# Windowed and coarse attention before two MLPs on one core: input loads put ahead of weights, value sums merged, and mask and spreading as matmuls for three half-batches

## The chip, the cores and the metric

The kernel runs on one core of a Trainium2 chip. The metric is device time in microseconds (us) from the start to the end of one execution; the median of several runs is given. The core has a matmul engine (TensorE, here PE, with its weight loads PEld), a vector engine (VectorE, DVE), a scalar engine (ScalarE, ACT), a general engine (GpSimd, POOL) and a queue engine (SyncE, SP) that issues transfers. PE writes its results to the accumulator memory PSUM; DVE and ACT read PSUM and the main on-chip memory SBUF. Each engine works through its own queue in order.

## What is computed

```python
B, H, S, D = 4, 8, 576, 64
def _attn_ref(q, k, v):
    factor = 4
    ...
    q_d = q.reshape(B, H, Sd, factor, D).mean(axis=3)      # likewise k_d, v_d
    out_d = sm_attn(q_d, k_d, v_d)
    out_up = np.repeat(out_d, factor, axis=2)
    mask = np.abs(pos[:, None] - pos[None, :]) < factor
    scores = scale * np.matmul(q, k.transpose(0, 1, 3, 2))
    scores = np.where(mask, scores, -1000000000.0)
    ...
    return (out_up + out_local).astype(np.float32)

def _moe_ref(x, w_in, w_out):                              # x: 2304 x 512, d_ff 2048
    h = x @ w_in
    return ((h * np.cos(h)) @ w_out).astype(np.float32)

def _moe2_ref(x, w_a, w_b, w_out):                         # d_ff 1536
    return ((x @ w_a) * (x @ w_b) @ w_out).astype(np.float32)

def reference(...):
    x = attn_out.transpose(0, 2, 1, 3).reshape(B * S, H * D)
    return _moe2_ref(x=_moe_ref(x, ...), ...)
```

An attention with two parts is followed by two MLPs. The local part lets each position see the three neighbours on either side; the coarse part runs a full attention over means of four positions, and each of its 144 results is repeated for four positions and added.

## The kernel before

The 2304 tokens are cut into eight half-batches u of 288 tokens (batch b, half of the sequence). The eight heads of a half-batch are taken as four pairs `hp`; two heads a = 0, 1 share the 128 partitions, 64 each.

For one pair, `down_sums` adds up four neighbouring columns of k and q, `local_scores` multiplies q and k in five windows of 64 positions into one PSUM tile (`att`), adds the mask with a DVE instruction (L214), takes the maximum (L218) and subtracts it (L219), and `down_scores` multiplies the summed q and k (L230). After the exponentials and the division (`local_norm`, `down_norm`) the weights are transposed on PE (`local_transpose`, `down_transpose`) and `attend` multiplies them with the values: four matmuls of 72 columns for the coarse part into columns 288 to 359 of the `att` tile (L315), ten for the windows into columns 0 to 287 (L322). `combine` copies the coarse result to SBUF on ACT (L332) and adds it, each column read four times, to the windows' result on DVE (L334); the sum `xf` is one 128-row block of x. `xsplit_hi` and `xsplit_lo` cut it into a high and a low half, `xh` (ACT) and `xl` (DVE, or POOL in u = 1 and 2). The values' sums over four positions, `vd`, are made by POOL in `sum_vs`, one head at a time: three additions of 72 x 128 elements from a tile `vs`.

Every product of the MLPs is made of three matmuls of 288 columns (`mm3`, L413 to L415) from high and low halves. A weight of 128 x 512 numbers comes as 64-bit floats of 0.5 MB (`wload`), and `wsplit` makes its halves: L107 and L111 on ACT, L108 and L109 on DVE, L112 on POOL. All 32 weights of the first MLP are split while its first four blocks run, at most eight loads ahead (`AHEAD`). A step g is one product `h` (one block of 128 hidden units for one half-batch), its `h cos(h)` on ACT and DVE (tile `gs`, L455 to L464), the halves `gh` and `gl`, and, three steps later, the four products `acc` with the second weight. The blocks run as u = 0 and u = 1 with hidden units 0 to 7, both with 8 to 15, and then u = 2 to 7 with all 16; the second MLP follows.

The attention of u = 0 stands ahead of the steps. That of u = 1 is spread over the first steps and that of u = 2 over steps 14 to 31, by tables of times `T1` and `T` (`unit_slots`); a planner then sorts each engine's instructions by what it expects to be ready, so that the order on an engine is not the order of the code. PSUM has two `att` tiles from u = 1 on; u = 0 borrows six more.

Of the kernel before, what the change touches and what calls it, by code (L numbers as in the profile page):

```python
# [36 lines left out]
C = {'AHEAD': 8, 'LEAD': 4, 'NPRE': 4, 'ND': 'ddd', 'XL': 'dpp', 'SUMS0': 'dddd', 'SUMS1': 'pppp', 'GLO': 8, 'FS': 8, 'S1': 0.7, 'G2': 14, 'LC': 0, 'DM': 2, 'LAG': 3, 'NGS': 3, 'MK': 0, 'SB': 'ddd', 'NL': 'dpp', 'W0': 0, 'W1': 0, 'W2': 0, 'W3': 0, 'NWV': 3, 'NGH': 4, 'XB': 8, 'YE': 6, 'CA': 2, 'NR': 4, 'PA': 1, 'LAG2': 2, 'PK': 1.0, 'GE': 'ad', 'NXF': 3, 'LP': 0, 'T': {'sums': [0, 0.5, 1.0, 3.0], 'ls': [0, 0, 0, 1.5], 'ds': [1, 1.5, 3, 4], 'ex': 6, 'ln': [6.0, 9.5], 'dn': [6, 7, 9, 10], 'dt': [7, 9.5, 11, 12], 'lt': [7.5, 8.5, 12.0, 13.5], 'at': [9.5, 9.5, 13.5, 14.5], 'xh': [11.0, 12.0, 15.0, 15.5], 'xl': [12.5, 13.5, 15.5, 15.5]}, 'T1': {'sums': [0, 0, 1.0, 2.0], 'ls': [0.5, 1.5, 2.5, 3.5], 'ds': [1, 1.5, 3, 4], 'ex': 5, 'ln': [5.5, 8], 'dn': [5.0, 6.0, 8.0, 9.0], 'dt': [6.0, 7.5, 10.0, 11.0], 'lt': [7.0, 8.0, 12.0, 12.0], 'at': [9, 9, 13, 14], 'xh': [9.0, 10.0, 13.0, 14.0], 'xl': [9.5, 11, 15, 15]}}  # L37
# [16 lines left out]
def kernel(ctx, tc, qT, kT, vw, vds, w_in, w_out, w_a, w_b, w_out2, out):  # L54
# [77 lines left out]
    def load_q(u, hp):  # L132
        if u < NU:
# [5 lines left out]
            sp.dma_start(out=t, in_=qT[b, hp, :, BASE[half]:BASE[half] + HALF])  # L139
            qt[u, hp] = t  # L140

    def load_v(u):
        for pr in range(HP // 2 if u < NU else 0):
# [539 lines left out]
```

## Time and profile before

| | |
|---|---|
| median of three runs | 1054.56 us (1050.47 to 1056.16) |
| the profiled execution | 1054.71 us, its span 1052.9 us |
| PE busy | 1009.0 us, 96% of the span |
| DVE, ACT, POOL busy | 543.1, 495.3, 188.1 us |
| moved by DMA | 72.97 MB |

The span runs from the first to the last instruction of the profiled execution. Busy time of PE is that of its matmuls; weight loads overlap them. An f32 matmul of the attention is recorded as two matmuls, so ten of them show as x20.

### The profile page before, as it was taken

The page shows a single profiled execution, that of the slowest core. Times are in us where ns is not written, and L with a number is a line of the kernel's source. Part 1 is how long each engine was busy: PE and PEld are TensorE (multiplying, and loading weights), DVE is VectorE, ACT ScalarE, POOL GpSimd, SP SyncE. Part 2 cuts the span into 40 slices and gives each one's busy share as a digit, 9 for nine tenths or more (in the row PEclk, how much of TensorE's full clock was granted, in tenths as well). Part 3 has the DMA queues.
Part 4 walks back from the last instruction along what each step waited for, and adds up shares of the span by engine and source line. Part 5 has one row for each costly group of instructions (what it writes and reads, how often), then busy time and mean ns, then how long its engine had stood idle before and what let it go on. Part 6 is the DMA issues. An engine that isn't in the chain of part 4 may idle for free.

```text
span 1052.9 us, 20576 instructions
## 1 busy us (share of the span) xinstructions
PE 1009.0 (96%) x8400; PEld 969.4 (92%) x8400; DVE 543.1 (52%) x1212; ACT 495.3 (47%) x1170; POOL 188.1 (18%) x215
## 2 busy tenths in 40 slices
PE   5978899999999999999999989999999999999998
PEld 4767789999999999999988979999999999999998
DVE  7788875674667756566488882222222222122211
ACT  4677766475665756657677562212121212122211
POOL 4868731000300003000033550000000001000000
PEclk9889999999999999999999999999999999999999
DMA  9545411301203012010174750001010102010000
GB/s 306 195 161 199 118 50 37 97 8 38 75 19 105 14 37 69 14 42 2 61 223 143 234 168 29 24 1 45 1 46 1 47 1 65 4 40 6 18 7 24
DMA packets 37919, 72.97 MB, mean 69 GB/s; under 512 B 4288, under 2 KB 22720, under 8 KB 37824
## 3 DMA queue, kind: packets, MB, share of 16 engines
q1 hardware_dynamic: 37824, 71.65, 21.3%
q8 instruction: 66, 1.08, 0.4%
q14 instruction: 29, 0.24, 0.1%
HBM read 61.01 MB, written 10.62 MB: 68 GB/s over the span
## 4 chain that ended last, share of the span: by engine, by line
PE 77%; POOL 6%; DVE 6%; issue 5%; DMA 3%; ACT 3%; SPq 0%; POOLq 0%; ACTq 0%; DVEq 0%
PE acc L413 10%; PE acc L414 9%; PE acc L415 9%; PE h L413 5%; PE h L414 5%; PE h L415 5%; PE pb L413 5%; PE pb L415 4%; PE pa L413 4%; PE pb L414 4%; PE pa L414 4%; PE pa L415 4%; POOL w L112 4%; PE att L322 2%; PE att L203 2%
## 5 line engine op out<-in xcount | busy, mean ns | idle before, releaser
L413 PE MATMUL acc<-gh,w 128*128 128x288 f32 x832 | 251.2, 302 | 2.0 <-DVE ev L449 1.5
L414 PE MATMUL acc<-gl,w 128*128 128x288 f32 x832 | 248.1, 298 | 3.5 <-DVE gl L472 1.7
L415 PE MATMUL acc<-gh,w 128*128 128x288 f32 x832 | 246.9, 297 | 0.0
L468 ACT ACTIVATE gh<-gs 128x288 fp32r<-128x288 f32 x224 | 99.3, 443 | 184.0 <-DVE gs L623 130.3
L623 DVE TENSOR_TENSOR gs<-a_sb,pb 128x288 f32<-128x288 f32 x96 | 43.5, 454 | 253.2 <-PE pb L415 253.2
L413 PE MATMUL h<-xh,w 128*128 128x288 f32 x512 | 159.0, 310 | 9.2 <-DVE gs L464 8.2
L413 PEld LDWEIGHTS acc<-gh,w 128*128 128x128 f32 x832 | 157.8, 190 | 7.0 <-issue 3.5
L414 PEld LDWEIGHTS acc<-gl,w 128*128 128x128 f32 x832 | 157.8, 190 | 5.6 <-DVE gl L472 2.9
L415 PEld LDWEIGHTS acc<-gh,w 128*128 128x128 f32 x832 | 157.9, 190 | 0.1
L415 PE MATMUL h<-xh,w 128*128 128x288 f32 x512 | 153.0, 299 | 1.4 <-POOL w L112 1.4
L472 DVE TENSOR_TENSOR gl<-gs,gh 128x288 fp32r<-128x288 f32 x216 | 115.7, 536 | 74.9 <-ACT gh L468 73.8
L414 PE MATMUL h<-xl,w 128*128 128x288 f32 x512 | 154.1, 301 | 0.0
L619 ACT COPY a_sb<-pa 128x288 f32<-128x288 f32 x96 | 38.3, 398 | 174.9 <-PE pa L415 174.8
L413 PEld LDWEIGHTS h<-xh,w 128*128 128x128 f32 x512 | 98.0, 191 | 16.6 <-DVE gs L464 14.2
L415 PEld LDWEIGHTS h<-xh,w 128*128 128x128 f32 x512 | 98.1, 192 | 1.7 <-POOL w L112 1.7
L414 PEld LDWEIGHTS h<-xl,w 128*128 128x128 f32 x512 | 98.0, 191 | 1.7 <-issue 1.7
L413 PE MATMUL pa<-xh,w 128*128 128x288 f32 x320 | 95.0, 297 | 2.5 <-ACT a_sb L619 2.5
L413 PE MATMUL pb<-xh,w 128*128 128x288 f32 x320 | 95.0, 297 | 2.2 <-DVE gs L623 2.2
L112 POOL TENSOR_TENSOR w<-raw,w 128x512 fp32r<-128x512 f32 x62 | 86.4, 1402 | 56.8 <-ACT w L111 56.6
L414 PE MATMUL pa<-xl,w 128*128 128x288 f32 x320 | 94.5, 295 | 0.0
L414 PE MATMUL pb<-xl,w 128*128 128x288 f32 x320 | 94.4, 295 | 0.0
L415 PE MATMUL pb<-xh,w 128*128 128x288 f32 x320 | 94.2, 294 | 0.0
(100 smaller groups left out, 1889.8 us busy)
## 6 DMA issues: line engine op xcount, KB each, us to landing
raw<-in_w_out_dram SPq DMA_DIRECT2D x28, 512.0 KB
raw<-in_w_in_dram SPq DMA_DIRECT2D x16, 512.0 KB
raw<-in_w_a_dram SPq DMA_DIRECT2D x12, 512.0 KB
raw<-in_w_b_dram SPq DMA_DIRECT2D x12, 512.0 KB
v<-in_vw_dram SPq DMA_DIRECT2D x16, 320.0 KB
q<-in_qT_dram SPq DMA_DIRECT2D x32, 146.0 KB
k<-in_kT_dram SPq DMA_DIRECT2D x16, 288.0 KB
vs<-in_vds_dram SPq DMA_DIRECT2D x32, 144.0 KB
```

Source lines behind the costliest of these rows:

```text
L112: lo_eng.tensor_tensor(out=t[:, 1], in0=lw.bitcast(F32), in1=t[:, 0].bitcast(F32), op=ALU.subtract)
L203: pe.matmul(p[r, W * w:W * w + W], qt[u, hp][r, off:off + W], kt[b, hp][r, BASE[half] + off:BASE[half] + off + W], start=not pem, stop=True,)
L322: pe.matmul(p[64 * a:64 * a + 64, xo:xo + n], vt[u, hp // 2][r, w, a], pt[u, hp // 2][r, w, 64 * a + qo:64 * a + qo + n], start=True, stop ...
L413: i = pe.matmul(ps_out, lh, rh, start=start, stop=False)
L414: pe.matmul(ps_out, lh, rl, start=False, stop=False)
L415: pe.matmul(ps_out, ll, rh, start=False, stop=stop)
L468: act.activation(out=gh[g], in_=gs[g], func=AF.Copy)
L472: eng.tensor_tensor(out=gl[g], in0=gs.pop(g), in1=gh[g].bitcast(F32), op=ALU.subtract)
L619: act.copy(out=a_sb, in_=pa)
L623: dve.tensor_tensor(out=gs[g], in0=a_sb, in1=pb, op=ALU.mult)
```

## The change

Six things change.

1. The loads ahead of the first step: SP issues the four key loads, one weight, two value tiles, a weight, and so on, and the query loads of u = 0 go to ACT's queue. Before, SP alternated keys, queries and four weights, and the value tiles came behind.
2. `load_vs` and `sum_vs` handle a pair of heads at a time: four transfers of 72 x 1024 numbers in place of eight of 72 x 512, and three additions of 72 x 256 elements in place of six of 72 x 128.
3. For u = 0 the sums of pairs 2 and 3 (`SUMS0`) go from DVE to POOL.
4. For u < 3 (`MK`) the mask is put into the PSUM tile by one bf16 matmul (identity times mask, 320 columns) ahead of the ten of q and k, which then add to it. The DVE addition L214 falls away, and maximum and subtraction read PSUM.
5. For u < 3 (`UP`) the coarse matmuls of `attend` read each weight column four times, and so write 288 columns where they wrote 72, straight into the columns of the windows' result, to which the window matmuls then add. `combine` only hands the PSUM tile on; `xsplit_hi` and `xsplit_lo` read it from PSUM, the latter on DVE for all of u < 3.
6. The queue memory kept for DMA descriptors is set to 1024 (`dynamic_dma_scratch_size`), and in u = 0 `local_scores` is written ahead of `down_sums`.

```diff
-C = {... 'SUMS0': 'dddd', ... 'MK': 0, ...}
+C = {... 'SUMS0': 'ddpp', ... 'MK': 3, 'UP': 3, ...}
...
-            o = vdt[b, hp][:, par]
+            t = vst.pop((u, hp))
+            o = vdt[b, hp] = at.tile([QD, 4, D], F32, tag="vd", name="vd", bufs=4)
             pool.tensor_tensor(out=o, in0=t[:, :, 0], in1=t[:, :, 1], op=ALU.add)
...
-                    start=not pem, stop=True,
+                    start=not pem, stop=not pem or w == NW - 1,
...
     def attend(u, hp):
+        up = u < C["UP"]
         for c in range(2):
             for a in range(2):
-                pe.matmul(
-                    p[64 * a:64 * a + 64, NB:NB + QD], vdt[b, hp][:, a, c], pd[u, hp][:, 2 * a + c],
-                    start=(c == 0), stop=(c == 1),
-                )
+                w = pd[u, hp][:, 2 * a + c]
+                o = p[64 * a:64 * a + 64, NB:NB + QD]
+                if up:
+                    o = p[64 * a:64 * a + 64, :NB].rearrange("p (s r) -> p s r", r=4)
+                    w = w.unsqueeze(2).to_broadcast([QD, QD, 4])
+                pe.matmul(o, vdt[b, hp][:, 2 * a + c], w, start=(c == 0), stop=(c == 1 and not up))
...
-                    start=True, stop=True,
+                    start=not up, stop=not up or w == NW - 1,
...
     def combine(u, hp):
         p = opsum.pop((u, hp))
+        if u < C["UP"]:
+            xf[u, hp] = p[:, :NB]
+            return
...
-                     (T["xl"][hp], xsplit_lo, u, hp, pick("XL", u))]
+                     (T["xl"][hp], xsplit_lo, u, hp, dve if u < C["UP"] else pick("XL", u))]
...
-            load_q(0, hp)
-            if hp < C["NPRE"]:
-                load_next(None)
-        for hp in range(HP):
-            for par in range(2):
-                load_vs(0, hp, par)
-        load_v(0)
-        for _ in range(C["AHEAD"] - C["NPRE"]):
+            load_q(0, hp, act)
+        load_next(None)
+        load_vs(0, 0)
+        load_vs(0, 1)
+        load_next(None)
+        load_v(0, 0)
+        load_vs(0, 2)
+        load_vs(0, 3)
+        load_v(0, 1)
+        for _ in range(C["AHEAD"] - 2):
             load_next(None)
         for hp in range(HP):
+            local_scores(0, hp)
             down_sums(0, hp)
-            local_scores(0, hp)
```

Three places show how the planner's orders move. DVE at the start of the program, before (`kd`, `qd` are sums of keys and queries, `mx`, `mxd` maxima, `raw` a weight):

```order
L176 TENSOR_REDUCE kd<-k 128x144
L176 TENSOR_REDUCE qd<-q 128x72
L232 TENSOR_REDUCE mxd<-att 72x1
L108 TENSOR_SCALAR raw<-raw 128x512
L176 TENSOR_REDUCE kd<-k 128x144
L176 TENSOR_REDUCE qd<-q 128x72
L109 SCALAR_TENSOR_TENSOR raw<-raw 128x512
L232 TENSOR_REDUCE mxd<-att 72x1
L214 TENSOR_TENSOR smx<-att,mask 128x5x64 x2
L218 TENSOR_REDUCE mx<-smx 128x5 x2
L219 TENSOR_TENSOR smx<-smx,mx 128x5x64 x2
L176 TENSOR_REDUCE kd<-k 128x144
```

and DVE at the same place after the change, where the lines have other numbers:

```order
L174 TENSOR_REDUCE qd<-q 128x72
L174 TENSOR_REDUCE kd<-k 128x144
L174 TENSOR_REDUCE qd<-q 128x72
L174 TENSOR_REDUCE kd<-k 128x144
L108 TENSOR_SCALAR raw<-raw 128x512
L216 TENSOR_REDUCE mx<-att 128x5
L109 SCALAR_TENSOR_TENSOR raw<-raw 128x512
L217 TENSOR_TENSOR smx<-att,mx 128x5x64
L216 TENSOR_REDUCE mx<-att 128x5
L230 TENSOR_REDUCE mxd<-att 72x1
L217 TENSOR_TENSOR smx<-att,mx 128x5x64
```

The mask additions are gone, maximum and subtraction take `att` (PSUM) as their source, and the sums of the third and fourth pair no longer stand here.

PE at the attends of u = 1 (`smd`, `vd` are the coarse weights and values, `smx`, `v` those of the windows), before:

```order
L315 MATMUL att<-smd,vd 64x72 x4
L322 MATMUL att<-smx,v 64x57 x6
L322 MATMUL att<-smx,v 64x56 x2
L322 MATMUL att<-smx,v 64x61 x2
L413 MATMUL h<-xh,w 128x288
L414 MATMUL h<-xl,w 128x288
L415 MATMUL h<-xh,w 128x288
L413 MATMUL h<-xh,w 128x288
L305 MATMUL att<-ident,smd 72x72 x4
```

and PE at the same place after:

```order
L319 MATMUL att<-smd,vd 64x288 x4
L323 MATMUL att<-smx,v 64x57 x6
L323 MATMUL att<-smx,v 64x56 x2
L323 MATMUL att<-smx,v 64x61 x2
L417 MATMUL h<-xh,w 128x288
L303 MATMUL att<-ident,smd 72x72 x4
L418 MATMUL h<-xl,w 128x288
L419 MATMUL h<-xh,w 128x288
```

The coarse matmuls are four times as wide, and the transpose of the third pair's coarse weights, which needs an `att` tile, comes one `h` matmul behind the attends instead of four.

POOL at the first value additions, before (`vs_120`, `vs_122` are the values of one head each):

```order
L169 TENSOR_TENSOR vd<-vs_120 72x128
L170 TENSOR_TENSOR vd<-vd,vs_120 72x128
L171 TENSOR_TENSOR vd<-vd,vs_120 72x128
L169 TENSOR_TENSOR vd<-vs_122 72x128
L170 TENSOR_TENSOR vd<-vd,vs_122 72x128
L171 TENSOR_TENSOR vd<-vd,vs_122 72x128
```

and POOL at the first value additions after (`vs_118`, `vs_120` are the values of one pair each, `q_114` the queries of the fourth pair):

```order
L167 TENSOR_TENSOR vd<-vs_118 72x256
L178 TENSOR_TENSOR kd<-kd,k 128x144
L168 TENSOR_TENSOR vd<-vd,vs_118 72x256
L169 TENSOR_TENSOR vd<-vd,vs_118 72x256
L167 TENSOR_TENSOR vd<-vs_120 72x256
L176 TENSOR_TENSOR qd<-q_114 128x72
L168 TENSOR_TENSOR vd<-vd,vs_120 72x256
L177 TENSOR_TENSOR qd<-qd,q_114 128x72
L169 TENSOR_TENSOR vd<-vd,vs_120 72x256
L178 TENSOR_TENSOR qd<-qd,q_114 128x72
```

The value additions are half as many and twice as wide, and key and query sums of the third and fourth pair stand ahead of them and between them; the cast of the mask to bf16 stands behind the first addition on the third pair's keys.

## Rows read from the trace of the kernel before

**Rows 1.** Windows: length, then busy us (instructions) per engine, granted clock, DMA.
```profile
core 0: us, PE busy (x) PEld busy (x) DVE busy (x) ACT busy (x) POOL busy (x), PEclk, DMA share, GB/s
0.00:34.00 34.00, 22.27 (x234) 17.35 (x234) 24.48 (x62) 16.98 (x48) 18.40 (x37) 1.00 0.91 309
20.00:34.00 14.00, 12.36 (x133) 9.99 (x133) 10.67 (x27) 7.43 (x22) 12.67 (x19) 1.00 0.92 356
34.00:140.00 106.00, 87.02 (x722) 77.13 (x719) 92.31 (x170) 76.10 (x179) 80.26 (x78) 0.89 0.45 148
140.00:320.00 180.00, 179.48 (x1690) 170.52 (x1690) 111.85 (x292) 113.40 (x271) 21.04 (x34) 1.00 0.15 45
```

**Rows 2.** PE's waits from 0 to 160 us: total, times, longest.
```profile
PE h L413 <- DVE gs L464: 7.4, 6, 2.0
PE att L203 <- DMA q<-in_qT_dram: 5.6, 2, 4.2
PE att L203 <- DVE smx L214: 2.6, 1, 2.6
...
PE acc L414 <- POOL gl L472: 1.7, 1, 1.7
...
PE h L415 <- POOL w L112: 1.4, 1, 1.4
PE att L296 <- POOL smx L274: 1.2, 1, 1.2
```

**Rows 3.** Chain that ended last, 30 to 40 us: start, length, what.
```profile
31.73 0.46 POOL vd L171
...
34.22 0.54 PE h L413
34.76 0.24 PE h L414
...
37.41 1.26 PE att L203 x20
```

**Rows 4.** Groups by shape, 0 to 320 us: busy us, mean ns, idle before.
```profile
L214 DVE TENSOR_TENSOR smx<-att,mask 128x320 f32<-128x320 f32 x20 | 9.5, 481 | 3.5 <-PE att L203 3.4
...
L176 DVE TENSOR_REDUCE kd<-k 128x144 f32<-128x576 f32 x12 | 8.9, 742 | 3.9 <-DMA k<-in_kT_dram 3.9
L334 DVE TENSOR_TENSOR xf<-att,up 128x288 f32<-128x288 f32 x19 | 8.6, 454 | 5.4 <-ACT up L332 5.4
...
L176 DVE TENSOR_REDUCE qd<-q 128x72 f32<-128x288 f32 x18 | 7.9, 440 | 0.0
```

**Rows 5.** The same view of 34 to 140 us, mask addition and subtraction.
```profile
L219 DVE TENSOR_TENSOR smx<-smx,mx 128x320 f32<-128x320 f32 x8 | 6.7, 841 | 0.0
...
L214 DVE TENSOR_TENSOR smx<-att,mask 128x320 f32<-128x320 f32 x8 | 3.8, 481 | 2.8 <-PE att L203 2.7
```

**Rows 6.** Timeline of DVE in the first stage: start, length, instruction.
```profile
17.52 0.48 DVE L214 TENSOR_TENSOR smx<-att,mask 128x320 f32<-128x320 f32 x1
...
18.74 0.48 DVE L219 TENSOR_TENSOR smx<-smx,mx 128x320 f32<-128x320 f32 x1
```

**Rows 7.** Timeline of the first stage, SP's queue and POOL's first value addition.
```profile
1.19 0.42 SPq L139 DMA_DIRECT2D q<-in_qT_dram  x1
...
15.60 1.08 POOL L169 TENSOR_TENSOR vd<-vs 72x128 f32<-72x128 f32 x1 [13.15 <-DMA vs<-in_vds_dram]
```

**Rows 8.** Timeline of PE at u = 1's attends, once cut off at 77.13 us.
```profile
76.61 0.29 PE L413 MATMUL h<-xh,w 128*128 128x288 f32 x1
76.74 0.29 PE L414 MATMUL h<-xl,w 128*128 128x288 f32 x1
76.97 0.35 PE L315 MATMUL att<-smd,vd 72*64 72x72 f32 x4
...
76.97 0.47 PE L315 MATMUL att<-smd,vd 72*64 72x72 f32 x8
77.37 0.80 PE L322 MATMUL att<-smx,v 64*64 64x57 f32 x20
```

**Rows 9.** Timeline of PE at an attend of u = 2.
```profile
183.83 0.47 PE L315 MATMUL att<-smd,vd 72*64 72x72 f32 x8
```

More of the change, by code (lines that the diff above doesn't have):

```diff
@@ L130, in load_k, with load_q @@
             kt[b, hp] = t
-    def load_q(u, hp):
+    def load_q(u, hp, eng=sp):
         if u < NU:
@@ L138, in load_q, with load_v @@
                 t = at.tile([128, HALF], F32, tag="q", name="q", bufs=3)
-            sp.dma_start(out=t, in_=qT[b, hp, :, BASE[half]:BASE[half] + HALF])
+            eng.dma_start(out=t, in_=qT[b, hp, :, BASE[half]:BASE[half] + HALF])
             qt[u, hp] = t
-    def load_v(u):
-        for pr in range(HP // 2 if u < NU else 0):
+    def load_v(u, *prs):
+        for pr in (prs or range(HP // 2)) if u < NU else ():
             if u == 0:
@@ L149, in load_v, with load_vs @@
             vt[u, pr] = t
-    def load_vs(u, hp, par):
+    def load_vs(u, hp):
         b, half = divmod(u, 2)
@@ L154, in load_vs, with sum_vs @@
             if u == 0:
-                t = wp.tile([QD, 2, 4, D], F32, tag="w", name="vs0", bufs=33)
+                t = wp.tile([QD, 4, 4, D], F32, tag="w", name="vs0", bufs=33)
             else:
-                t = at.tile([QD, 2, 4, D], F32, tag="vs", name="vs", bufs=1)
-            ins = sp.dma_start(out=t, in_=vds[b, 2 * hp + par])
+                t = at.tile([QD, 4, 4, D], F32, tag="vs", name="vs", bufs=1)
+            ins = sp.dma_start(out=t, in_=vds[b, hp])
             after(ins, gate.get(u))
-            vst[u, hp, par] = t
-    def sum_vs(u, hp, par):
+            vst[u, hp] = t
+    def sum_vs(u, hp):
         b, half = divmod(u, 2)
         if half == 0:
-            t = vst.pop((u, hp, par))
-            if par == 0:
-                vdt[b, hp] = at.tile([QD, 2, 2, D], F32, tag="vd", name="vd", bufs=4)
-            o = vdt[b, hp][:, par]
+            t = vst.pop((u, hp))
+            o = vdt[b, hp] = at.tile([QD, 4, D], F32, tag="vd", name="vd", bufs=4)
             pool.tensor_tensor(out=o, in0=t[:, :, 0], in1=t[:, :, 1], op=ALU.add)
@@ L362, in unit_slots @@
         todo += [(15, load_v, u + 1)]
-        for i in range(H):
-            todo += [(i, load_vs, u, i // 2, i % 2), (i + 2, sum_vs, u, i // 2, i % 2)]
+        for hp in range(HP):
+            todo += [(2 * hp, load_vs, u, hp), (2 * hp + 3, sum_vs, u, hp)]
         order = [load_vs, sum_vs, load_q, load_k, down_sums, local_scores, down_scores, exps, local_norm, down_norm, local_transpose,
@@ L521 @@
         for hp in range(HP):
-            for par in range(2):
-                sum_vs(0, hp, par)
+            sum_vs(0, hp)
         for hp in range(HP):
@@ L535 @@
             xsplit_hi(0, hp)
-            xsplit_lo(0, hp, pick("XL", 0))
+            xsplit_lo(0, hp)
         load_v(1)
@@ L652, in _layout @@
                 vw[u, hp // 2, hp % 2, :, w] = v[b, 2 * hp:2 * hp + 2, s0:s0 + W].transpose(1, 0, 2)
-    vds = v.reshape(B, H, 2, QD, 4, D).transpose(0, 1, 3, 2, 4, 5)
+    vds = v.reshape(B, HP, 2, 2, QD, 4, D).transpose(0, 1, 4, 2, 3, 5, 6).reshape(B, HP, QD, 4, 4, D)
     return {
@@ L668 @@
     laid = _layout(**{n: _np.asarray(a) for n, a in inputs.items()})
-    nc = _bacc.Bacc("TRN2", target_bir_lowering=False, num_devices=1)
+    nc = _bacc.Bacc("TRN2", target_bir_lowering=False, num_devices=1, dynamic_dma_scratch_size=1024)
     arrays, args = {}, []
```

2 lines of the change are left out of this document (1 added, 1 removed).

## Prediction

> **What bounds the kernel now.** Read the windows view first [rows 1]. From 140 to 320 us the matmul engine (PE) is busy 179.48 of 180 us: nothing but PE's own work counts from there on. What can be won lies before 140 us. In the first 34 us PE is busy 22.27 us; from 34 to 140 us it is busy 87.02 of 106 us at a mean granted clock of 0.89, while VectorE (DVE) is busy 92.31, ScalarE (ACT) 76.10 and GpSimd (POOL) 80.26. The busiest engine besides PE is DVE, and the list of waits says the same: PE's longest total wait before 160 us is for DVE's `gs` at L464 (7.4 us in six waits), with 2.6 us more for DVE's mask add L214, against 1.4, 1.7 and 1.2 us for POOL's L112, L472 and L274 [rows 2]. The chain of work shows the first stage: POOL's value sums follow one another until 32.2, the last attend waits for them, and the first `h` product starts at 34.22 [rows 3]. DVE is no less tied there: busy 24.48 of 34 us [rows 1], 3.9 us of the rest waiting for keys [rows 4]. So the first stage has two limits side by side, and both must move.
>
> **DVE's relief.** Durations are from the groups by line and shape [rows 4].
> First half-batch (u = 0): four mask adds go (L214, 4 x 0.481 = 1.9), four adds of the spread result (L334, 4 x 0.454 = 1.8), and two pairs' key and query sums move to POOL (2 x (0.742 + 0.440) = 2.4). Together 6.1 us.
> u = 1: four mask adds 1.9 and four L334 1.8 go, but the four low halves of x come to DVE from POOL; I price them at L334's 0.45, since both read one operand from PSUM, so +1.8. Net 1.9 us.
> u = 2: mask adds 1.9 us. Its L334 fall after 140 us, where DVE has time to spare, and are worth nothing.
> The subtraction of the maximum (L219) now reads PSUM instead of SBUF. Between 34 and 140 us the eight of u = 1 and 2 took 841 ns each, while the eight L214, whose large operand is in PSUM, took 481 ns beside the same POOL work [rows 5]. In the first stage two neighbours are equal, 0.48 and 0.48 [rows 6]. So the subtraction is long there because both operands are in SBUF while POOL works; I take 481 ns for it, 8 x 0.36 = 2.9 us. Bounds: 0, if the other DVE instructions take over the waiting, and 2.9.
> Sum for DVE: 6.1 + 1.9 + 1.9 + 2.9 = 12.8 us.
> [...]
>
> **POOL and the loads.** The value sums now start when the first value tile lands. SP issued four weights and all keys and queries ahead of them, and the first sum waited 13.15 us, until 15.60 [rows 7]. Now one weight stands ahead of them. The 24 sums of 128 elements took from 15.60 to 32.2, at 0.46 us where nothing held them (31.73 [rows 3]); twelve of 256 elements should take 0.45 to 0.9 us each, between one of 128 elements and two of them, so 5.4 to 10.8 us. POOL also takes twelve small adds for two pairs' sums, about 0.45 each like the 128-element adds, 5.4 us. Even with the long ends, and starting at about 6 us, POOL is through by some 22 us, ten before the 32.2 of now. Its first weight comes earlier by that much, so the wait of `h` for L112 (1.4 us) goes: -1.4. Bounds 0 and 4.3 (all three waits for POOL [rows 2]). The weights loaded later are hardly missed: ahead of the third one stand 3.5 MB of inputs and two weights of 0.5 MB, and with its own 0.5 MB at the 309 GB/s of the first 34 us [rows 1] it lands at some 16 us, while DVE's new order has 39 rows ahead of it.
> For the queries that move to ACT's queue I count nothing. PE's waits for `q` are 5.6 us, the longest 4.2 [rows 2], and SP's issue of one load takes 0.42 [rows 7], so at most 4 x 0.42 = 1.7 us of issuing is saved. [...]
>
> **PE's price.** The mask matmul is nearest to an `h` matmul (288 columns, 0.13 us from start to start at the high clock, 76.61 to 76.74 [rows 8]); with its load of weights about 0.2 us each, twelve of them 2.4, all before 140 us, where PE is idle 11.7 of the first 34 us and 19.0 of the next 106 [rows 1]: 0, and 2.4 if that cover is gone. The first masks wait for POOL's cast, behind an addition on the third pair's keys; DVE has four sums (2.4 us) and L108 of the first weight ahead of its first maximum, so 0 again.
> The spreading makes four f32 matmuls of each pair of heads 288 columns wide instead of 72. At the high clock the block of four (eight records) starts at 76.97 and the next kind at 77.37, 0.40 us; inside it four further records add 0.12 us (0.35 for four, 0.47 for eight [rows 8]), so about 0.25 us grows with the columns. Four times that is 1.0: +0.75 us per pair of heads. Bounds: 0 if the loads of weights set the pace, +1.2 if the whole 0.40 grows fourfold. [...]
> u = 0: 4 x 1.5 = 6.0 us between the first attend and the first `h`. PE is busy 12.36 of the 14 us from 20 to 34 [rows 1], so 1.6 us are free: the rest, 4.4, shows (bounds 1.4, at the high clock, and 6.0). PE is what is late next: behind the attends in its queue stand `h` and the scores of u = 1, and DVE waits for those, though it has weights to split meanwhile.
> u = 1: 4 x 0.75 = 3.0, between 34 and 140 us; PE's 19.0 idle us there cover it: 0, and 3.0 if they are gone.
> u = 2: its attends lie around 184 us [rows 9], where PE has no gap: 3.0 us in full.
> The accumulators now hold PSUM until x's low half is made, but DVE's new order has those right behind the high halves at the places of the old adds; 0, up to 2 us in u = 1, where a transpose now stands one `h` matmul behind the attends instead of four.
> **Sum:** -12.8 - 1.4 + 4.4 + 0 + 3.0 = -6.8 us. The profiled execution took 1054.71 us (span 1052.9), the median is 1054.56, so nothing has to be shifted: 1054.7 - 6.8 = 1047.9.
>
> **The rivals.**
> *Relief not passed on.* ACT (76.10) and POOL (80.26 of 106 us [rows 1]) are nearly as full as DVE, and cos steps need all of them in turn. If half of the 6.7 us from 34 to 140 is kept and no wait for POOL falls away: -6.1 - 3.3 + 4.4 + 3.0 = -2.0, 1052.7. Against it: PE's waits for DVE's `gs` and L214 sum to 10.0 us, those for POOL to 4.3 [rows 2].
> *Slower: the wide matmuls do not overlap in pairs.* The two heads of a pair write different halves of the partitions. If they run one after another at 288 columns, the growing part is 2.0 instead of 1.0 and the price 1.75 per pair of heads (3.5 at the low clock): u = 0 14.0 - 1.6 = 12.4, u = 1 half hidden 3.5, u = 2 7.0, and -14.2: +8.7, 1063.4. It decides from a price of about 1.1 (no gain) and 1.5 (slower by half a per cent) on. Against it: records come 0.03 us apart at 72 columns.
> *More: the clock rises in the attends.* Longer streams keep PE busier from 22 us on. At the high clock u = 0 shows 3.0 - 1.6 = 1.4, and with all three waits for POOL gone: -12.8 - 4.3 + 1.4 + 3.0 = -12.7, 1042.0. Against it: PE was busy 12.36 of 14 us before 34 us and without a gap from there to 37.41, and the clock stayed low [rows 1, 3].
> *Nothing of it acts.* The orders show that the instructions move, so this is small.
>
> **How the numbers follow.** 0.5% (5.3 us, a line at 1049.3) is about what a measurement of this kernel can tell from no change. The forecast gets 0.42, with a range of its own of 1042 to 1053 from its bounds (waits for POOL, subtraction, u = 1); about three quarters of it, 0.32, lie below 1049.3. The larger gain gets 0.15, all faster. The relief not passed on gets 0.28, 0.26 of it within 0.5%. The unpaired matmuls get 0.15, 0.13 of it slower. Faster 0.48, same 0.38, slower 0.14. For eight in ten the range leaves out the far ends of the larger gain and of the unpaired case: 1041 to 1060.
>
> **What would show it.** POOL's last value sum for u = 0 before 24 us; spreading blocks of about 1.15 us at the high clock and 2.2 at the low; the first `h` product done no more than 4 us after 37.4; subtractions near 0.48 us from 34 to 140; PE's waits for DVE's `gs` below 7.4 us; PE full from some ten microseconds earlier than 140, and around u = 2's attends 3 us more PE work. The prediction is wrong if that block takes over 1.5 us at the high clock, if PE waits for the attends' accumulators in u = 1, or if ACT or POOL take over DVE's place as what PE waits for.

## The result, and the profile after

The changed kernel takes 1067.95 us in the median of four runs (1066.37 to 1069.55); the kernel before, run beside it, takes 1054.07. The ratio is 1.0135 with a 95% interval of 1.0103 to 1.0168. The change is **slower by about 14 us**, where 6.8 us less were forecast, and the time lies outside the range of 1041 to 1060 us.

The profiled execution took 1066.37 us, its span is 1064.5 us, 11.6 more than before. The first part of the page gives busy time, share of the span and instructions of each engine:

```profile
span 1064.5 us, 20499 instructions
...
PE 1020.5 (96%) x8412; PEld 971.5 (91%) x8412; DVE 536.7 (50%) x1192; ACT 494.1 (46%) x1158; POOL 168.3 (16%) x173
```

By these two lines the whole loss is busy time of PE: 1009.0 us before, 1020.5 now, +11.5. What is left of the span is PE's idle time, 1052.9 - 1009.0 = 43.9 us before and 1064.5 - 1020.5 = 44.0 now. So the relief of the other engines took nothing from PE's idle time. Busy time is not work alone, though: an `h` matmul is busy 0.29 us at the higher level of the clock [rows 8] and 0.44 at the lower (42.13 us in the timeline below). DVE lost only 6.4 us of work (543.1 to 536.7).

The windows, with the columns of [rows 1], for the same stretches:

```profile
0.00:34.00 34.00, 20.93 (x193) 13.77 (x193) 24.65 (x57) 16.92 (x46) 22.18 (x44) 0.78 0.87 309
34.00:140.00 106.00, 88.18 (x695) 74.11 (x692) 83.61 (x143) 70.63 (x162) 69.04 (x59) 0.81 0.44 148
140.00:320.00 180.00, 179.58 (x1646) 167.98 (x1645) 109.93 (x293) 111.28 (x263) 11.81 (x14) 1.00 0.15 45
```

From 34 to 140 us DVE is busy 83.61 us instead of 92.31 and POOL 69.04 instead of 80.26, but PE stands idle 17.8 us where it stood idle 19.0. DVE's idle time there rose from 13.7 to 22.4 us: the time that DVE was relieved of became its own idle time. PE's instructions in that stretch went from 722 to 695, at a mean granted clock of 0.81 instead of 0.89. (The 0.89 is a little too high: up to 36.7 us the `h` matmuls of the kernel before follow one another at 0.24 us, the lower level, where the column prints 1.00.)

PE's timeline at the attends (start, length, instruction, and in brackets the idle time before it and what ended it). The first four of the spreading blocks belong to u = 0, the next four to u = 1, the last is the first of u = 2's four:

```profile
23.30 2.19 PE L319 MATMUL att<-smd,vd 72*64 72x288 f32 x8
26.67 2.19 PE L319 MATMUL att<-smd,vd 72*64 72x288 f32 x8
32.36 2.19 PE L319 MATMUL att<-smd,vd 72*64 72x288 f32 x8
35.74 2.19 PE L319 MATMUL att<-smd,vd 72*64 72x288 f32 x8
...
42.13 0.44 PE L419 MATMUL h<-xh,w 128*128 128x288 f32 x1
42.50 1.33 PE L201 MATMUL att<-k,q 64*64 64x64 f32 x18
...
65.52 0.90 PE L294 MATMUL att<-ident,smx 128*128 128x128 f32 x3 [5.71 <-POOL smx L272]
...
68.62 2.19 PE L319 MATMUL att<-smd,vd 72*64 72x288 f32 x8
72.00 2.19 PE L319 MATMUL att<-smd,vd 72*64 72x288 f32 x8
81.06 1.19 PE L319 MATMUL att<-smd,vd 72*64 72x288 f32 x8
82.91 1.19 PE L319 MATMUL att<-smd,vd 72*64 72x288 f32 x8
...
174.83 1.19 PE L319 MATMUL att<-smd,vd 72*64 72x288 f32 x8
```

A block takes 1.19 us at the higher of the clock's two levels and 2.19 at the lower (the clock column prints 1.00 from 82 to 84 us and 0.50 from 22 to 46); the narrow block took 0.47 at the higher [rows 8, 9]. Six of the twelve run at the low level, two of them in u = 1. The point that answers to 37.41 us in [rows 3], where the first `h` product is done and the scores of u = 1 follow, is now 42.50. And PE now stops 5.71 us before the transposes of u = 1, where the kernel before waited 1.2 [rows 2].

The list of PE's waits from 0 to 160 us, the same view as [rows 2]:

```profile
PE att L228 <- DVE kd L174: 6.6, 1, 6.6
PE h L417 <- DVE gs L468: 6.5, 5, 1.9
PE att L294 <- POOL smx L272: 5.7, 1, 5.7
PE att L228 <- POOL qd L178: 3.5, 1, 3.5
PE att L197 <- DVE smx L217: 3.1, 1, 3.1
PE att L303 <- DVE smd L287: 3.0, 1, 3.0
```

The waits have other names, and their sum is no smaller (PE is idle 30.9 us up to 140 us, before 30.7). The wait for `gs`, on which the forecast had built, went from 7.4 to 6.5 us.

### The profile page after: what moved, and what is told of

It is laid out like the page before. It is cut to its first block, busy times and chain, and to the rows that moved or that the text cites. A ratio compares the mean times of both kernels' runs of the same rounds, so it can differ in the third digit from the quotient of the medians.

```text
span 1064.5 us, 20499 instructions
## 1 busy us (share of the span) xinstructions
PE 1020.5 (96%) x8412; PEld 971.5 (91%) x8412; DVE 536.7 (50%) x1192; ACT 494.1 (46%) x1158; POOL 168.3 (16%) x173
## 3 DMA queue, kind: packets, MB, share of 16 engines
q1 hardware_dynamic: 35904, 71.05, 20.8%
## 4 chain that ended last, share of the span: by engine, by line
PE 80%; DVE 7%; ACT 4%; issue 3%; DMA 2%; POOL 2%; SPq 0%; DVEq 0%; POOLq 0%; ACTq 0%
PE acc L417 10%; PE acc L418 9%; PE acc L419 9%; PE h L417 6%; PE h L418 5%; PE h L419 5%; PE pb L417 5%; PE pb L419 4%; PE pa L417 4%; PE pb L418 4%; PE pa L419 4%; PE pa L418 4%; DVE raw L109 3%; PE att L319 2%; PE att L323 2%
## 5 line engine op out<-in xcount | busy, mean ns | idle before, releaser
L472 ACT ACTIVATE gh<-gs 128x288 fp32r<-128x288 f32 x224 | 99.2, 443 | 187.1 <-DVE gs L628 130.1
L417 PEld LDWEIGHTS h<-xh,w 128*128 128x128 f32 x512 | 98.6, 193 | 15.7 <-DVE gs L468 12.6
L112 POOL TENSOR_TENSOR w<-raw,w 128x512 fp32r<-128x512 f32 x62 | 87.8, 1423 | 69.5 <-ACT w L111 68.8
```

Source lines behind the costliest of these rows:

```text
L112: lo_eng.tensor_tensor(out=t[:, 1], in0=lw.bitcast(F32), in1=t[:, 0].bitcast(F32), op=ALU.subtract)
L417: i = pe.matmul(ps_out, lh, rh, start=start, stop=False)
L472: act.activation(out=gh[g], in_=gs[g], func=AF.Copy)
```

## Experiments

The questions: what is the relief worth, what do the wide matmuls cost and in which half-batch, and why doesn't the one pay for the other. **Theory A** says that what PE is given to do shows in the time and that the relief isn't passed on. Its rivals are a wait for the sums moved to POOL (B), accumulators held by the masked scores (C), loads and merged sums (D), and later ones. Each run was timed beside the kernel before on the same chip; 0.001 of a ratio is 1.05 us. PE idle and DVE idle are those of 34 to 140 us in the profiled execution (106 us less the busy time of the window).

Two things limit what a row can tell. The planner sorts the queues anew for every edit, so a run differs from its neighbour in the order of many instructions besides the edit: in e13, where the edit only repeats additions of the mask, DVE's order leaves that of the kernel before at the 74th instruction and PE's at the 270th. No run holds the order still, so an effect of a few us may be one of the order. And the columns on the right come from one execution, which need not be near the median: e10's took 1063.21 us, the slowest of seven (median 1059.05), e8's 1060.06, the slowest of twelve (1055.52).

| run | ratio (95% interval) | span less PE busy, all | PE idle | DVE idle |
|---|---|---|---|---|
| before | 1 | 43.9 | 19.0 | 13.7 |
| changed | 1.0135 (1.0103 to 1.0168) | 44.0 | 17.8 | 22.4 |
| e1 no spreading | 1.0026 (1.0013 to 1.0040) | 43.3 | 17.4 | 16.6 |
| e2 no mask matmuls | 1.0162 (1.0142 to 1.0182) | 49.0 | 19.5 | 18.6 |
| e3 neither | 1.0022 (1.0007 to 1.0037) | 46.4 | 17.6 | 13.2 |
| e4 spreading in u = 1, 2 | 1.0112 (1.0092 to 1.0131) | 47.8 | 21.0 | 21.7 |
| e5 relief alone | 1.0046 (1.0031 to 1.0062) | 47.6 | 18.8 | 20.9 |
| e6 spreading twice | 1.0243 (1.0222 to 1.0265) | 38.0 | 12.6 | 31.4 |
| e7 spreading in u = 2 | 1.0054 (1.0037 to 1.0072) | 44.6 | 17.4 | 14.8 |
| e8 e1, norm on DVE | 1.0032 (1.0017 to 1.0047) | 45.7 | 18.1 | 18.3 |
| e9 e5, sums on DVE | 1.0015 (1.0000 to 1.0030) | 46.4 | 19.8 | 22.6 |
| e10 mask matmuls alone | 1.0056 (1.0035 to 1.0077) | 44.6 | 16.1 | 21.4 |
| e11 e1, sums on DVE | 1.0042 (1.0026 to 1.0058) | 47.2 | 20.7 | 17.4 |
| e12 changed, sums on DVE | 1.0126 (1.0098 to 1.0154) | 45.1 | 18.5 | 21.2 |
| e13 mask added thrice | 1.0043 (1.0030 to 1.0056) | 46.6 | 20.8 | 10.4 |
| e14 no bit merge | 0.9941 (0.9929 to 0.9954) | 39.8 | 13.8 | 31.2 |

**e1, no spreading matmuls.** In the table of numbers of the changed kernel:
```diff
-'UP': 3
+'UP': 0
```


> The coarse result goes back to its own 72 columns and is spread by VectorE and GpSimd; mask matmuls, merged sums, the two sums on GpSimd and the new order of loads stay. Theory A (the loss is what the spreading blocks cost TensorE in its low-clock stretches, 17 to 46 and 65 to 80 us, with ScalarE and VectorE standing behind the split of x): the 13.9 us go, 1050 to 1056 us, and the first h product ends at 38 us or sooner instead of 42.5. Rival B (the sums of pairs 3 and 4 on GpSimd open a gap of 3.5 us before the scores, and TensorE's clock falls there): that gap stays, 1064 to 1069 us. Rival C (masked scores read straight from PSUM hold the attention buffers, 3.1 us of TensorE's waits): 1064 us or more. Rival D (loads or merged sums): 1066 to 1070 us.

Measured 1054.81 us, ratio 1.0026: all but 2.7 us of the loss went. The wait for POOL's sums is still there (4.2 us at 17.16 us), so B as the main cause falls. C and D fall as main causes too, since the mask matmuls, the loads and the merged sums are all still in this kernel.

**e2, no mask matmuls.**
```diff
-'MK': 3
+'MK': 0
```


> The mask is added by VectorE again in all half-batches; spreading matmuls, sums and loads stay as changed. Theory A: VectorE gets back 12 adds of 0.84 us less 12 subtractions' gain, in stretches where it had become idle, so 1066 to 1073 us, no better than the changed kernel. Rival C (attention buffers held by the masked scores): the wait of 3.1 us at 130 us and some of the lag go, 1060 to 1065 us. Rivals B and D: 1068 to 1074 us.

Measured 1069.01 us, ratio 1.0162, as by A. (The adds take 0.48 us each, as in [rows 4], not the 0.84 of the expectation.) The mask matmuls are no loss here; beside the spreading they gain about 2.8 us, which the intervals do not settle; beside e3's kernel nothing (next run).

**e3, neither.** Both edits together.

> Neither mask matmuls nor spreading matmuls; left of the change are the order of loads, the merged sums, and the sums of pairs 3 and 4 on GpSimd. Theory A: 1052 to 1058 us, at the kernel before or little off. Rival B: 1062 to 1068 us, with the wait of the coarse scores for GpSimd's sums (3.5 us) still there and the low clock behind it. Rival D: 1062 to 1070 us. Rival C: 1054 to 1060 us, as by A; this run doesn't tell A from C.

Measured 1054.28 us, ratio 1.0022, against 1.0026 with mask matmuls: taking twelve mask adds from DVE and giving twelve matmuls to PE makes no difference that can be measured. Loads, merged sums and the two pairs' sums on POOL together cost 2.3 us (0.7 to 3.9). In the profile PE is idle 15.0 of the first 34 us, where it was idle 11.7 before [rows 1].

**e4, spreading in the second and third half-batch only.**
```diff
-C = {... 'UP': 3, ...}
+C = {... 'UPS': (1, 2), ...}
...
-        up = u < C["UP"]
+        up = u in C["UPS"]
...
-        if u < C["UP"]:
+        if u in C["UPS"]:
```
The choice of the engine for `xsplit_lo` changes in the same way.


> Spreading matmuls in the second and third half-batch only; the first goes back to VectorE's and GpSimd's spreading. Theory A in its first form (the loss is made in the first half-batch, at the low clock before the first h product): 1054 to 1058 us. Theory A in its second form (the loss is made once the products have begun, where blocks and low clock sit in the second and third half-batch): 1062 to 1067 us, only the 5.1 us by which the first h product is late come back at most. Rivals B, C and D: 1065 to 1069 us.

Measured 1063.65 us, ratio 1.0112: the second form. Most of the loss is made after the first half-batch.

**e7, spreading in the third alone.** The same edit with `'UPS': (2,)`.

> Spreading matmuls in the third half-batch alone. Theory A: 4 x 0.75 us at the high clock over the kernel without spreading matmuls (1054.8 us), 1057 to 1059 us; the second half-batch's part is then the rest of the 8.9 us of the two together, 5.9 us, twice as much for the same columns at half the clock. Rival G (the price isn't TensorE's columns but the accumulators held longer, or the split of x done by VectorE): the same price in each half-batch, 4.4 us, 1058.5 to 1060.5 us.

Measured 1058.13 us, ratio 1.0054, 2.9 us above e1. By differences of ratios the three half-batches cost u = 2 2.9, u = 1 (e4 less e7) 6.1, u = 0 (changed less e4) 2.4 us; each is uncertain by 2 to 4 us. Rival G's equal price of 4.4 isn't excluded by them alone. The traces tell more. Each step g is 12 `h` matmuls, so the start of the 241st marks step 20, behind the attention of u = 1 and ahead of u = 2's attends: 148.2 us in e1, 148.6 in e7, 155.3 in e4, 157.0 in the changed kernel. So in these executions u = 1 costs 6.7 us and u = 0 1.6. From there to step 32, behind u = 2's attends, e1 takes 46.3 us and the three others 49.2: 2.9 us for u = 2. That is not one price. The blocks in e4's timeline of PE show a part of the reason: half of them stand at the low clock in u = 1.

```profile
65.98 2.19 PE L319 MATMUL att<-smd,vd 72*64 72x288 f32 x8 [1.19 <-ACT smx L296]
69.35 2.19 PE L319 MATMUL att<-smd,vd 72*64 72x288 f32 x8
79.11 1.19 PE L319 MATMUL att<-smd,vd 72*64 72x288 f32 x8
...
80.96 1.19 PE L319 MATMUL att<-smd,vd 72*64 72x288 f32 x8
```

Against 0.75 and 0.47 us for narrow blocks that is 2 x 1.44 + 2 x 0.72 = 4.3 us of PE's time for u = 1, 4 x 0.72 = 2.9 for u = 2 (the measured value) and 4 x 1.44 = 5.8 for u = 0: 13.0 us in all. The narrow 0.75 is from e7's timeline, at the same place and clock:

```profile
66.20 0.75 PE L319 MATMUL att<-smd,vd 72*64 72x72 f32 x8 [1.18 <-ACT smx L296]
```

**e5, the relief alone.**
```diff
-'UP': 3
+'UP': 0
...
-            pe.matmul(p[:, :NW * W].rearrange("p (w k) -> p w k", k=W), identb, maskb.unsqueeze(1).to_broadcast([128, NW, W]), start=True, stop=False)
+            pass
...
-                    start=not pem, stop=not pem or w == NW - 1,
+                    start=True, stop=True,
...
     def combine(u, hp):
         p = opsum.pop((u, hp))
-        if u < C["UP"]:
+        if u < 3:
             xf[u, hp] = p[:, :NB]
             return
...
-                     (T["xl"][hp], xsplit_lo, u, hp, dve if u < C["UP"] else pick("XL", u))]
+                     (T["xl"][hp], xsplit_lo, u, hp, dve if u < 3 else pick("XL", u))]
```


> The relief without its price: in the first three half-batches the mask isn't added at all and the coarse result isn't spread (it is computed in 72 columns and left unused); so the adds leave VectorE, the spreading adds leave VectorE and the copies ScalarE, while TensorE gets no mask matmul and no wide matmul. The split of x stands on VectorE as in the changed kernel. Theory A, now: the relief is not passed on to TensorE, and what TensorE is given to do costs its full time; 1052 to 1056 us. Rival E (the relief is worth what was forecast, 12.8 us, and the spreading matmuls cost more than twice what was forecast): 1040 to 1046 us. Between them, 1047 to 1051 us: the relief is passed on in part.

Measured 1056.40 us, ratio 1.0046: not even the kernel before is reached. The relief is there and PE has no work for it, but nothing is gained. Rival E falls. The windows of the first 34 us and of 34 to 140 us, and from the lists of waits in the second those of DVE, ACT, POOL and PE:

```profile
0.00:34.00 34.00, 19.33 (x236) 15.58 (x236) 23.96 (x55) 16.81 (x47) 18.68 (x38) 0.71 0.85 310
34.00:140.00 106.00, 87.16 (x698) 76.90 (x699) 85.08 (x156) 72.81 (x171) 71.33 (x66) 0.82 0.44 150
...
DVE mxd L230 <- PE att L228: 5.9, 5, 3.4
DVE gs L468 <- ACT gs L467: 5.2, 5, 1.8
DVE gs L460 <- ACT gs L459: 3.9, 4, 2.3
...
ACT gh L472 <- DVE gs L468: 7.8, 5, 3.1
ACT gs L459 <- PE h L419: 6.7, 3, 3.4
...
POOL w L112 <- ACT w L111: 29.7, 16, 9.9
...
PE h L417 <- DVE gs L468: 5.9, 6, 2.3
```

In the first 34 us PE is idle 14.7 us, before 11.7 [rows 1]; from 34 to 140 us 18.8, as before. Read as a ring: PE waits for DVE's `gs`, DVE waits for ACT to make the input of `gs`, ACT waits for PE's `h`, and POOL waits for ACT. In the kernel before, the same lists name 2.3 us for DVE's wait for L459's counterpart and 11.2 us for POOL's wait for ACT. So the time taken off DVE is spent there in waiting for its neighbours. That is a reading of the lists; no run shortens one link of the ring and leaves the order alone.

**e9, the same with all sums of u = 0 on DVE.**
```diff
-'SUMS0': 'ddpp'
+'SUMS0': 'dddd'
```


> As the run with the relief alone (no mask added and no coarse result spread in the first three half-batches, no matmul in their place), with all four pairs' sums of the first half-batch on VectorE again, as before. Theory A (the relief becomes idle time of VectorE, whoever makes the first sums): 1051 to 1056 us, and VectorE's idle time between 34 and 140 us at or above the 20.9 us of the run with the relief alone. Rival J (the relief is worth its 12.8 us, but TensorE's wait for GpSimd's sums at 17 us, 3.2 to 4.2 us, and the clock behind it ate it): 1040 to 1047 us.

Measured 1054.72 us, ratio 1.0015: as by A. Rival J, that a wait for POOL's sums ate the relief, falls: 12.8 us do not come back. But e9 is 3.3 us faster than e5, and the two intervals don't overlap. PE's idle time in the first 34 us is 12.6 us instead of 14.7. So without mask matmuls moving the two pairs' sums to POOL costs time.

**e12 and e11, the changed kernel and e1 with the sums on DVE.** The same edit.

> The changed kernel with all four pairs' sums on VectorE. Theory A (price of the spreading matmuls): 1064 to 1069 us, within 3 us of the changed kernel. Rival B (GpSimd's sums open the gap in which the clock falls, and that is the loss): 1054 to 1061 us.

> No spreading matmuls; mask matmuls, merged value sums and new loads as changed, the four pairs' sums on VectorE as before. Theory A: TensorE's wait of 4.2 us for GpSimd's sums at 17 us goes, VectorE gets 2.3 us of sums back at its busiest place (10 to 20 us): 1050 to 1055 us, at most 2 us better than with GpSimd's sums. If it comes out under 1049 us, it beats both kernels, and the sums were what the other parts' gain was lost to.

Measured 1066.49 us (1.0126) and 1057.98 us (1.0042). The first is the changed kernel within the intervals, so B is out there as well. The second came out 1.7 us above e1 by the ratios and 3 us above the top of what was expected: with the mask matmuls in the kernel the sums may stand on either engine.

**e8, e1 with u = 1's local weights normalized by DVE.**
```diff
-'NL': 'dpp'
+'NL': 'ddp'
```


> No spreading matmuls; mask matmuls, merged sums and new loads as changed; in addition the second half-batch's local weights are normalized by VectorE instead of GpSimd. Theory A (between 55 and 65 us TensorE waits for the chain from exponentials over VectorE's sums to GpSimd's product, 4.5 us, and that chain, not VectorE's busy time, sets what it waits): 1051 to 1054 us, with the wait shorter by 2 us or more. Rival H (VectorE is the bound there, each us given to it costs a us): 2 x 0.9 us more, 1056 to 1058 us.

Measured 1055.52 us, ratio 1.0032, the same as e1. Between the two expectations, and so inconclusive: the wait at the transposes fell from 4.5 to 3.7 us, and other waits took it back (in the slowest of its twelve executions).

**e10, the kernel before with the mask matmuls alone** (and the changed kernel's `dynamic_dma_scratch_size=1024`).
```diff
-'MK': 0
+'MK': 3
...
-                    start=not pem, stop=True,
+                    start=not pem, stop=not pem or w == NW - 1,
```


> The kernel before with the mask matmuls of the first three half-batches alone: loads, sums and spreading as before. Theory A: the relief of 12 adds isn't passed on and the 12 matmuls of the mask cost TensorE about 0.2 us each at most: 1051 to 1055 us, a ratio of 0.998 to 1.004. Forecast's terms (relief passed on, mask matmuls hidden): 12 adds of 0.48 us and 3.4 us of dearer subtractions fewer, 1043 to 1049 us.

Measured 1059.05 us, ratio 1.0056: worse than either expectation. PE's timeline starts so:

```profile
8.65 0.76 PE L230 MATMUL att<-kd,qd 64*72 64x144 f32 x4 [8.65 <-DVE qd L176]
9.34 0.45 PE L199 MATMUL att<-maskb,identb 128*128 128x320 bf16 x1
```

The first local scores stand behind the mask, and PE begins at 8.65 us, not at 4.23, where its wait of 4.2 us for `q` ended before [rows 2]. In the changed kernel it begins at 6.60 (the wait for `kd` above), and without a mask matmul, in e5, at 4.25 as before. The late start was forecast to cost nothing. With it PE has 7.8 us more busy time (1016.8 against 1009.0), more than twelve mask matmuls of 0.45 us, 5.4 in all at most. The profiled execution is the slowest of e10, and its granted clock from 34 to 140 us is 0.80, before 0.89; a longer time at the lower level could account for the rest, but no run separates it.

**e6, each spreading block twice.**
```diff
-        for c in range(2):
+        for i in range(4 if up else 2):
+            c = i % 2
             for a in range(2):
...
-                pe.matmul(o, vdt[b, hp][:, 2 * a + c], w, start=(c == 0), stop=(c == 1 and not up))
+                pe.matmul(o, vdt[b, hp][:, 2 * a + c], w, start=(c == 0), stop=(c == 1 and not (up and i == 3)))
```


> Each spreading block is issued twice, the second time over the first; the result is the same. Theory A (every column given to TensorE costs its time in full, nothing of it lies in TensorE's idle time): 8 more blocks of 2.12 us at the low clock and 4 of 1.15 at the high one, 21.6 us, so 1087 to 1092 us. Rival F (half of it or more fits into the 17.8 us in which TensorE is idle between 34 and 140 us, and the loss comes from elsewhere): 1068 to 1079 us.

Measured 1077.89 us, ratio 1.0243: 11.4 us above the changed kernel, not 21.6. Theory A in its strict form falls, and F holds for the second copy. The busy times on e6's page:

```profile
PE 1037.2 (96%) x8508; PEld 979.3 (91%) x8508; DVE 529.8 (49%) x1192; ACT 494.1 (46%) x1158; POOL 170.6 (16%) x173
```

PE's busy time rose by 16.7 us, and its idle time fell by 6.0 (44.0 to 38.0). So of added PE work about two thirds showed here (11.4 of 16.7). For the first copy it is 9.4 (changed less e5) to 11.5 us (changed less e1) of 13.0.

**e13 and e14: what DVE's time is worth in the kernel before.** Still open was whether DVE's busy time doesn't count from 34 to 140 us, or whether this relief came at the wrong places. e13 adds to it, e14 takes away more than twice the forecast relief.

```diff
-            dve.tensor_tensor(out=sm, in0=src, in1=mask.unsqueeze(1).to_broadcast([128, NW, W]), op=ALU.add)
+            for _ in range(3 if u in (1, 2) else 1):
+                dve.tensor_tensor(out=sm, in0=src, in1=mask.unsqueeze(1).to_broadcast([128, NW, W]), op=ALU.add)
```


> The kernel before, with the mask's add issued three times over in the second and third half-batch (the same values each time): 16 adds of 0.48 us, 7.7 us more for VectorE between 34 and 140 us, nothing else changed. Theory K (VectorE has slack there: the engines wait for each other in a fixed order, and its busy time is not what sets TensorE's waits in either direction): 1052 to 1056 us. Rival L (VectorE is the bound from 34 to 140 us, and the relief failed only for other reasons): 1058 to 1063 us. A rise without an equal fall under relief would say: an added us on the chain to the scores counts, a removed one meets the next engine's wait.

```diff
-        ins = dve.scalar_tensor_tensor(out=lw, in0=hh, scalar=3, in1=lw, op0=ALU.logical_shift_left, op1=ALU.bitwise_or)
+        if p2 is not None:
+            ins = dve.scalar_tensor_tensor(out=lw, in0=hh, scalar=3, in1=lw, op0=ALU.logical_shift_left, op1=ALU.bitwise_or)
```


> The kernel before without VectorE's merge of a weight's two bit fields in the first MLP (the weights are then nearly zero): 29 operations of 0.93 us, 26.7 us less for VectorE between 34 and 140 us and 3.8 us less ahead of it, more than twice what the change was to relieve it of, with no work given to TensorE. Rival L (VectorE's busy time is the bound from 34 to 140 us): the 19 us in which TensorE stands idle there shrink by 10 us or more, 1036 to 1045 us. Theory K: another engine's step takes its place in the ring, and no more than 5 us are gained, 1049 to 1056 us.

e14's edit reaches further than its expectation says: the second MLP's later weights are split without `p2` too, so 62 of the 68 merges go, and DVE's busy time falls by 43.0 us in the whole span (543.1 to 500.1). Some 30.5 us of that stood ahead of 140 us, and PE's idle time behind 320 us is 11.8 us, before 12.6, so little was gained behind it.

e13: 1057.29 us, ratio 1.0043, +4.5 us (3.2 to 5.9) for 7.7 us. e14: 1046.44 us, ratio 0.9941, -6.2 us (4.8 to 7.5) for 30.5 us. Neither K nor L in its pure form: an added microsecond cost 0.6, a removed one gave at most 0.2, each with the planner's new order in it. From e14's window and lists of waits (its line numbers are one higher than those of before from L110 on):

```profile
34.00:140.00 106.00, 92.25 (x764) 83.17 (x763) 74.77 (x148) 77.84 (x189) 73.01 (x82) 0.84 0.44 151
...
DVE gs L457 <- ACT gs L456: 10.1, 8, 2.4
...
ACT gs L456 <- PE h L416: 12.2, 7, 5.3
```

DVE is busy 17.5 us less than before [rows 1], and PE's idle time fell by 5.2 (19.0 to 13.8). DVE's wait for ACT's `gs` input went from 2.3 to 10.1 us: a good part of the relief has turned into a wait.

No version among these beats the kernel before with the full computation; e14, which does, leaves part of it out.

## Why the prediction was wrong

**The failed step: "DVE's relief ... 12.8 us", and "-1.4" for POOL.** These two terms were to give 14.2 us. e5, which has both and nothing of the price, measured +4.8 us (3.3 to 6.5). That is a miss of 19.0, nearly all of the 21.0 between the forecast -6.8 and the measured +14.2. The rest is the price: 9.4 us by the step from e5 to the changed kernel, where 7.4 were forecast. By the other path, over e1, loads, sums and mask stand at +2.7 and the price at 11.5; the half-batches below are told by that path. Of e5's +4.8, 3.3 us go when the two pairs' sums return to DVE (e9, +1.6); their move was forecast as 2.4 us of relief. Of the -1.4, the wait for POOL's L112 did go (the changed kernel's list names none), but waits of 5.7 and 3.5 us for POOL's `smx` and `qd` came in its place, though DVE stays what PE waits for longest. Two things were wrong about DVE's relief.

First, a busy engine and a list of waits were taken for a bound. DVE was busy 92.31 of 106 us, and PE's longest wait was for it; from this each microsecond less on DVE was counted as one less for PE. e13 and e14 measured the rate: 0.6 for a microsecond more, 0.2 for one less; e5 and e9 measured none for this relief. By the lists of waits PE waits for the end of a chain that runs through ACT, DVE and POOL and back to PE, and what DVE no longer needs, it waits for ACT and PE. The rival "Relief not passed on" named this, with the right reason ("cos steps need all of them in turn"), but kept half of the gain.

Second, even the relief was half as large. The parts that the traces show came as forecast: the additions are gone, and the subtraction that reads PSUM takes 0.48 us. But DVE's total fell by 6.4 us, not 12.8. In the groups of DVE from 34 to 140 us, first before and then after (the mean is the number behind the comma), the weights' split got slower:

```profile
L109 DVE SCALAR_TENSOR_TENSOR raw<-raw 128x512 uint32<-128x512 uint32 x29 | 26.7, 929 | 1.4 <-ACT raw L107 1.4
L108 DVE TENSOR_SCALAR raw<-raw 128x512 uint32<-128x512 uint32 x27 | 18.1, 685 | 1.9 <-DMA raw<-in_w_in_dram 1.3 <-DMA raw<-in_w_out_dram 0.6
```

```profile
L109 DVE SCALAR_TENSOR_TENSOR raw<-raw 128x512 uint32<-128x512 uint32 x25 | 25.8, 1043 | 0.2
L108 DVE TENSOR_SCALAR raw<-raw 128x512 uint32<-128x512 uint32 x24 | 19.4, 816 | 0.0
```

25 x 0.114 + 24 x 0.131 = 6.0 us: the bound "0, if the other DVE instructions take over the waiting" was the right end, and it held for more than the subtraction. Why they got longer no run here separates. That single ones are long isn't particular to this change: up to 140 us L109 takes 666 to 1853 ns before, with a median of 694, and 676 to 2119 after, with a median of 684. Nor is it shown that the subtraction's 841 ns before came from operands in SBUF beside a working POOL, as the forecast argued: of those eight, three took 0.48 us, and two of the three, at 40.14 and 46.45 us, ran beside POOL's L178, L472 and L112.

**The clock beside it.** The clock adds a swing of its own. In e1 the 97th `h` matmul, the first of step 8, starts 7.0 us earlier than before. First before, then e1:

```profile
92.02 0.40 PE L413 MATMUL h<-xh,w 128*128 128x288 f32 x1 [2.03 <-DVE gs L464]
```

```profile
85.01 0.40 PE L417 MATMUL h<-xh,w 128*128 128x288 f32 x1 [0.17 <-DVE gs L468]
```

About as many matmuls of PE lie ahead of it (632, before 624), but they are busy 63.92 us instead of 68.60. As an `h` matmul is busy 0.29 us at the higher level of the clock and 0.44 at the lower, less busy time for about equal work is read as more time at the higher level: so much are 4.7 of the 7.0 us, and only 2.3 are idle time. At step 20 nothing of the lead is left (148.24 against 147.82 us), and busy time up to there is 118.1 against 117.1 us. A lead of a few us on the way is therefore no sign yet that a relief is passed on.

**Reading PSUM.** In the changed kernel both forms of the subtraction stand side by side, with their maximum, in the groups by shape from 0 to 320 us:

```profile
L216 DVE TENSOR_REDUCE mx<-att 128x5 f32<-128x320 f32 x12 | 5.8, 483 | 4.1 <-PE att L201 4.1
L217 DVE TENSOR_TENSOR smx<-att,mx 128x320 f32<-128x320 f32 x12 | 5.8, 480 | 0.0
...
L217 DVE TENSOR_TENSOR smx<-smx,mx 128x320 f32<-128x320 f32 x8 | 3.9, 484 | 0.0
...
L216 DVE TENSOR_REDUCE mx<-smx 128x5 f32<-128x320 f32 x8 | 3.8, 479 | 0.1
```

From PSUM 483 and 480 ns, from SBUF 479 and 484. So neither takes longer from PSUM here, and it was right to add nothing for it to the sum.

**u = 0: "the rest, 4.4, shows".** Measured 2.4 us by differences of ratios (4.3 by the medians, 1.6 by the traces), with the blocks at the low clock as forecast. No row or run shows the 1.5 us a block that the forecast's 6.0 is made of; measured are 2.19 us for a wide block at the low clock (changed) and 0.75 for a narrow one (e7), 1.44 more a block, and `h` matmuls that start 0.24 us apart there and 0.13 at the higher level [rows 3, 8]. Behind them the first `h` product is 5.1 us later (37.41 to 42.50), against at most 4 expected. ACT's queue shows what stands behind: the high half of x waits for the attend, with the split of the weights behind it, and DVE and POOL wait in turn.

```profile
35.85 0.41 ACT L346 ACTIVATE xh<-att 128x288 fp32r<-128x288 f32 x1 [2.51 <-PE att L323]
36.16 0.66 ACT L111 ACTIVATE w<-raw 128x512 fp32r<-128x512 f32 x1
36.30 0.46 DVE L350 TENSOR_TENSOR xl<-att,xh 128x288 fp32r<-128x288 f32 x1 [2.36 <-ACT xh L346]
...
36.90 1.61 POOL L112 TENSOR_TENSOR w<-raw,w 128x512 fp32r<-128x512 f32 x1 [4.19 <-ACT w L111]
```

**u = 1: "PE's 19.0 idle us there cover it: 0".** Wrong, and the price was too low besides. Half of its blocks run at the low clock, so 4.3 us and not 3.0, and the measured cost is 6.1 us, 6.7 by the traces. That no idle time covered it is measured; the reason is argued: the idle time lies where PE waits for a chain, and the attends lie on that chain (transposes, attend, split of x, `h`), so that a longer block moves the next wait. What makes the cost larger than the blocks' 4.3 us is open. e6 shows a limit: of 16.7 us more, 6.0 went into idle time.

**u = 2: "3.0 us in full".** Right: 2.9 us by the ratios (e7 over e1) and by the traces, in a stretch where PE has no gap.

**Right besides:** PE's waits for `gs`, 6.5 us and so below 7.4, though nothing followed from it; the block (1.19 us against 1.15, 2.19 against 2.2), and so the rival of unpaired matmuls is out, although its time was near; the value sums on POOL, whose last ends at 23.3 us, under the 24 named; the loads moved to ACT's queue, which bring next to nothing: the first scores of e5 wait for `q` until 4.25 us, before until 4.23, and only a second wait of 1.4 us (5.6 less 4.2 [rows 2]) is gone, less than the 1.7 allowed. Wrong besides: PE was to be full ten microseconds before 140 us. From 130 to 140 us it is busy 6.94 of 10:

```profile
130.00:140.00 10.00, 6.94 (x54) 6.15 (x54) 5.59 (x13) 3.03 (x8) 3.63 (x4) 0.83 0.11 29
```

**Open:** which step of the ring has to be shortened for PE's idle time before 140 us to fall. e8 and e11 tried two and failed. Not settled either is what makes up the 2.3 us that loads, merged sums and the sums on POOL cost (e3); its trace has 3.3 us more idle time of PE in the first 34 us, and e9 against e5 points at the sums on POOL, but e11 against e1 does not.

## What to carry to other kernels

A list of waits names the engine that came last, not what a microsecond of it is worth: before counting relief of another engine as time, add some work to it and take some away, and read the rate, which here was 0.6 up, 0.2 down, and nothing for the change at hand. Where PE is busy for 96% of the span, work moved to PE is paid for in the main, here with two thirds to nine tenths of its length (11.4 of 16.7, and 9.4 to 11.5 of 13.0 us), even in a stretch with 18% idle time. The first check of a relief is busy time and idle time of the bound engine apart: here +11.5 and +0.1. And where a planner sorts the queues, an experiment should keep the order fixed, or its result holds a new order too.

## What was not expected of the hardware

DVE's split of the weights slowed down while POOL's busy time beside it fell (L109 929 to 1043 ns, POOL 80.26 to 69.04 us from 34 to 140 us). And the granted clock stands at its low level for much of 34 to 140 us in all these kernels (a printed mean of 0.79 to 0.86 in all but before, with 0.89), though PE is busy there 80 to 88% of the time; the same block costs 2.19 us at 68.62 and 1.19 at 81.06, 12 us later. A price taken from a place at one level must be asked for at which level the new place will be.
